# State products of the even heads on 48 instead of 64 columns of the turned keys, and one state bank that is cleared once

## The chip, the core and the metric

The kernel runs on one core of one Trainium2 chip. Times are microseconds on the device. The kernel before was measured three times: 484.71, 484.76 and 485.75 us, so the median is 484.76 us. One further execution was profiled. All durations below come from its trace.

## What is computed

An RWKV6 attention block is followed by an MLP mixer. The attention works on 4 sequences of 768 tokens, with 8 heads of 48 numbers each. For every head it carries a 48 x 48 state from token to token:

```
cur = einsum('bhd,bhe->bhde', u * k[t], v[t])
y[t] = einsum('bhd,bhde->bhe', r[t], state + cur)
state = w[t][..., None] * state + einsum('bhd,bhe->bhde', k[t], v[t])
```

The result, laid out as 4 x 768 x 384, goes through two matrix products over tokens and two over channels, each pair with a ReLU between them and a residual sum behind it.

## The kernel before

The attention is done in chunks of 64 tokens. A *unit* is 256 tokens of one sequence, so there are 12 units, three for each sequence. In a unit, `ends`, `keys`, `begins` and `queries` (L426 to L442) multiply the running products of `w` into the keys and queries. `tokens` (L471) then calls `turned_keys` (L337), which turns the keys so that the tokens stand on the partitions. `carry` (L486) calls `outer` (L352), which makes the products of turned keys and values. `update` and `scaled` (L492 to L512) carry the state from chunk to chunk, and `before` (L514) and `after` (L522) make the output.

Heads are kept in pairs. The even head of a pair has its 48 numbers on partitions 0 to 47 and the odd head on 64 to 111 (`P = 64`, `ROWS = 112`). Partitions 48 to 63 are padding, which holds zeros in the keys.

`turned_keys` turns each pair with a matmul against the identity (L343), and ScalarE copies 112 columns for each of four pairs out of PSUM into `kT` (L344). In a pair's 112 columns, 0 to 47 belong to the even head, 48 to 63 are padding and 64 to 111 belong to the odd head.

`outer` multiplies, for each pair of heads `a`, group of 128 tokens `c`, chunk `j` in it and head `q` of the pair, the turned keys (the operand that is loaded into the array) with 48 columns of values (the operand that streams through). The loaded operand takes the array's upper half of rows for `j` = 0 and the lower for `j` = 1, and the left half of columns for `q` = 0 and the right for `q` = 1. So the array works as four corners, one for each (j, q), and successive products go to different corners. The order is (0,0), (1,1), (0,1), (1,0). The even head loads 64 columns, its 48 and the 16 of padding. So it also writes partitions 48 to 63 of the state bank `kv_ps`, with zeros. The odd head loads 48 columns:

```
rows = slice(q * P, P + q * D)
```

A unit has 32 such products, or 24 in the last unit of a sequence, where the last chunk's state isn't needed. Each float32 product stands in the trace as two weight loads and two matmuls, called passes below: 8 units x 64 + 4 x 48 = 704 rows of each kind at L361.

In the first sequence, the state is carried in PSUM. ScalarE scales the state out of the bank (L497), and a matmul with the identity adds it back (L504) on all 112 rows. In later sequences VectorE adds it in SBUF (L512). Both read the padding rows too, which is why those must hold finite numbers. The bank comes from a pool of one buffer (`ps_a`), newly allocated in every `outer`, and once more by `back` (L893) of the first sequence's mixer.

The order of the work is written out by hand. For the first sequence it is the long `strict(...)` call (L1033). Later, `interleaved` (L1013) merges the pieces of the mixer of one sequence and of the attention of the next by the digits of `WEAVES`. Every engine works off its instructions in this order. ScalarE's first pieces are `masks` (L205), then `own_u` of unit 0 (L444, which issues at L329).

Of the kernel before, what the change touches and what calls it, by code (L numbers as in the profile page):

```python
# [10 lines left out]
f32 = mybir.dt.float32  # L11
# [9 lines left out]
B, H, S, D = 4, 8, 768, 48  # L21
DM = H * D
T = 64
C = S // 128
UC = 2
UB = C // UC
NU = B * UB
A = H // 2
P = 64
ROWS = P + D  # L30
# [35 lines left out]
def rwkv6_then_mixer(  # L66
# [18 lines left out]
    pe, dve, act, pool, sp = nc.tensor, nc.vector, nc.scalar, nc.gpsimd, nc.sync  # L85
# [32 lines left out]
    apool = ctx.enter_context(tc.tile_pool(name="apool", bufs=2))  # L118
# [4 lines left out]
    ps_a = ctx.enter_context(tc.tile_pool(name="ps_a", bufs=1, space=bass.MemoryType.PSUM))  # L123
# [3 lines left out]
    def bank(name):  # L127
        return ps_m.tile([128, 512], f32, name=name, tag="m")
# [18 lines left out]
    ident = const.tile([128, 128], f32, name="ident")  # L147
# [40 lines left out]
    load_w(0)  # L188
    act.dma_start(u_col, u)

    dve.memset(starts, 0.0)
    dve.memset(least, LEAST)
    dve.memset(most, -MOST)
# [11 lines left out]
    def masks():  # L205
        for j in range(2):
            act.copy(on_diagonal[ts(j, T)], ident[ts(j, T), ts(j, T)])
        act.copy(diagonal, on_diagonal)
        act.copy(before_it, strictly)

    wtok1 = wts.tile([128, C, DTOK], f32, name="wtok1")
    wtok2 = wts.tile([128, DTOK // 128, S], f32, name="wtok2")
# [123 lines left out]

    def turned_keys(k_):  # L337

        kT = apool.tile([128, UC, A, 128], f32, name="kT", bufs=1)
        both = [bank("k_ps").rearrange("p (a t) -> p a t", a=A) for c in range(UC)]  # L340
        for c in range(UC):
            for a in range(A):
                pe.transpose(both[c][:, a, :ROWS], k_[:ROWS, ts(c * A + a, 128)], ident[:ROWS, :ROWS])  # L343
        return kT, [lambda c=c: act.copy(kT[:, c, :, :ROWS], both[c][:, :, :ROWS]) for c in range(UC)]  # L344

    def all_turned(k_):
        kT, copies = turned_keys(k_)
        for f in copies:
            f()
        return kT  # L350

    def outer(kT, vt, half):  # L352

        kv = ps_a.tile([128, 2, 512], f32, name="kv_ps", tag="a")
        begun = set()
        for c in range(UC):
            for a in range(A):
                for j, q in ((0, 0), (1, 1), (0, 1), (1, 0)):
                    if 2 * (half * UC + c) + j < 2 * C - 1:
                        rows = slice(q * P, P + q * D)  # L360
                        pe.matmul(kv[rows, j, ds((c * A + a) * D, D)], kT[ts(j, T), c, a, rows],  # L361
                                  vt[ts(j, T), c, ts(2 * a + q, D)], start=(q, j) not in begun, stop=True, skip_group_check=True)
                        begun.add((q, j))
        return kv
# [40 lines left out]
    def unit(i):  # L405
# [80 lines left out]
        def carry():  # L486
            L["kv"] = outer(L.pop("kT"), vs[i], half)
# [61 lines left out]
    def slot(name, i, n=1):  # L549
        return room(name, *ROOMS[name])[:, ds(i * SLOT, n * SLOT)]  # L550
# [18 lines left out]
    def low_of_pair(kind, n):  # L569
        return source(kind, n) if kind else by_pair(kind, slot("forms3", 2 * n, 2))  # L570
# [52 lines left out]
    def left(kind, jt):  # L623
        up, joint = (by_pair(kind, form_of(kind, jt // 2, which)) for which in ("up", "joint"))
        if kind == 0:
            return [[t[:, m, ts(jt % 2, 128)] for m in range(3)] for t in (up, joint)]
        return [t[:, jt % 2] for t in (up, joint)]

    def join(to, high, low):
        dve.scalar_tensor_tensor(to, high.bitcast(f32), 1.0 / BASE, low.bitcast(f32), op0=ALU.mult, op1=ALU.add)  # L630
# [249 lines left out]
    def mixing(bt, x_of, out_rows, rounded=False):  # L880
        h1 = mpool.tile([128, DTOK // 128, DM], f32, name="h1", bufs=1)
        xT = mpool.tile([128, DM // 128, S], f32, name="xT", tag="xT", bufs=1)
        zs, sums = {}, {}

        def hidden(i, c):
            if c == 0:
                sums[i] = ps_m.tile([128, DM], f32, name="h1_ps", tag="m")
            pe.matmul(sums[i], now["wtok1"][:, c, ts(i, 128)], x_of()[:, c, :], start=(c == 0), stop=(c == C - 1))

        def rectified(i):  # L890
            act.activation(h1[:, i, :], sums.pop(i), AF.Relu)

        def back(c):  # L893
            if rounded and c == 0:
                ps = ps_a.tile([128, 2, 512], f32, name="h_ps", tag="a")[:, 0, :DM]
            else:
                ps = ps_m.tile([128, DM], f32, name="h_ps", tag="m")
            for i in range(DTOK // 128):
                pe.matmul(ps, now["wtok2"][:, i, ts(c, 128)], h1[:, i, :], start=(i == 0), stop=(i == DTOK // 128 - 1))
            x = x_of()  # L900
            dve.tensor_add(x[:, c, :], x[:, c, :], ps)

        def last_x():
            return [slot("x_forms", 2 * n, 2).rearrange("p (m t) -> p m t", m=3) for n in range(3)]

        def turn(c):

            ps = bank("xT_ps")[:, :DM].rearrange("p (m t) -> p m t", t=128)
            for m in range(DM // 128):
                pe.transpose(ps[:, m, :], x_of()[:, c, ts(m, 128)], ident)  # L910
            if not rounded or c < 4:
                act.copy(xT[:, :, ts(c, 128)], ps)
                return
            high, low, joint = (t[:, :, ts(c - 4, 128)] for t in last_x())
            act.mul(high, ps, UPWARD)
            dve.tensor_sub(low, ps, high.bitcast(f32))
            join(joint, high, low)

        def up(s, jt, blocks=range(DM // 128)):
            if jt == 0 and 0 in blocks:  # L920
                zs[s] = now["z"][int((bt, s) != (0, 0))].rearrange("p (j t) -> p j t", j=NJ)
            if 0 in blocks:
                sums["z", s] = ps_m.tile([128, SEG], f32, name="z_ps", tag="m")
            ps = sums["z", s]
            if rounded and s == 2:
                first, last = left(0, jt)
                low = low_of_pair(0, jt // 2)[:, :, ts(jt % 2, 128)]
                for n, (of, to) in enumerate(zip((first, [low[:, m] for m in range(3)], last), last_x())):
                    for m in range(3):
                        pe.matmul(ps, of[m], to[:, m], start=(n, m) == (0, 0), stop=(n, m) == (2, 2))  # L930
                act.activation(zs[s][:, jt, :], ps, AF.Relu, scale=1.0 - 1.0 / BASE)
                return
            for m in blocks:
                pe.matmul(ps, now["wch1"][:, m, ts(jt, 128)], xT[:, m, ts(s, SEG)],  # L934
                          start=(m == 0), stop=(m == DM // 128 - 1))
            if DM // 128 - 1 in blocks:
                act.activation(zs[s][:, jt, :], ps, AF.Relu)

        def down(s, n, jts):

            if jts[0] == 0:
                sums[n] = ps_m.tile([128, DM], f32, name="h2_ps", tag="m")
            ps = sums[n]
            for jt in jts:
                pe.matmul(ps, zs[s][:, jt, ts(n, 128)], now["wch2"][:, jt, :], start=(jt == 0), stop=(jt == NJ - 1))  # L945
            if jts[-1] == NJ - 1:
                o = mpool.tile([128, 2, DM], f32, name="o", bufs=1) if n == 0 else sums["o"]
                sums["o"] = o
                dve.tensor_add(o[:, n], x_of()[:, 2 * s + n, :], ps)
                sp.dma_start(out_rows(2 * s + n), o[:, n])  # L950

        return dict(hidden=hidden, rectified=rectified, xT=xT, back=back, turn=turn, up=up, down=down)

    now["z"] = halves
# [58 lines left out]
    def interleaved(order, *streams):  # L1013
# [17 lines left out]
    s0, s1, s2 = (e["updates"] for e in (e0, e1, e2))  # L1031
    t0, t1, t2 = (e["scaled"] for e in (e0, e1, e2))
    strict(lambda: load_part(0, 1), masks, e0["ends"], e0["own_u"][0], e0["own_u"][1], e0["own_u"][2], e0["own_u"][3], e0["begins"],  # L1033
           lambda: load_part(0, 0), e0["keys"], lambda: load_part(1, 1), e0["own_gram"], lambda: load_v(0), e0["ranges"][0], lambda: load_w(1),
           e0["tokens"], e0["queries"], e1["own_u"][0], e1["own_u"][1], e0["copied"][0], lambda: load_w(2), e0["gram"], e1["ends"], e0["copied"][1],
# [117 lines left out]
    def by_halves(b):  # L1153
# [17 lines left out]
        for half in range(UB):  # L1171
# [13 lines left out]
            for l in range(LEVELS):  # L1185
# [8 lines left out]
                decay = longer  # L1194
            by = decay[:ROWS].rearrange("p (x j) -> p x j", j=2)
            kv = outer(all_turned(k_), vt, half)
            for c in range(UC):
                for j in range(2):
# [82 lines left out]
```

## Time and profile before

| | |
|---|---|
| median of three runs | 484.76 us |
| span of the profiled execution | 484.2 us |
| TensorE matmul / weight load busy | 468.0 us (97%) / 411.1 us (85%) |
| VectorE / ScalarE / GpSimd busy | 336.4 / 254.3 / 59.3 us |
| matmuls of L361 in all (704) | 15.1 us with 64 columns, 13.5 us with 48 (they overlap) |
| ScalarE's copies to `kT` (24) | 12.1 us |

PE stands for TensorE's matmuls, PEld for its weight loads, DVE for VectorE, ACT for ScalarE, SP for the engine that issues most transfers. A row of groups names the line, the engine, the operation and the tiles (out<-in), for PE the rows and columns of the array that are used (64*48), then shapes and count. A row of the timeline begins with the start and the duration in us. A row of the chain of waits says which work ended last at each time. PEclk is the share of TensorE's full clock that was granted. It reads 1.00 where the trace has no record yet, at the very start.

### The profile page before, as it was taken

The page shows a single profiled execution, that of the slowest core. Times are in us where ns is not written, and L with a number is a line of the kernel's source. Part 1 is how long each engine was busy: PE and PEld are TensorE (multiplying, and loading weights), DVE is VectorE, ACT ScalarE, POOL GpSimd, SP SyncE. Part 2 cuts the span into 40 slices and gives each one's busy share as a digit, 9 for nine tenths or more (in the row PEclk, how much of TensorE's full clock was granted, in tenths as well). Part 3 has the DMA queues.
Part 4 walks back from the last instruction along what each step waited for, and adds up shares of the span by engine and source line. Part 5 has one row for each costly group of instructions (what it writes and reads, how often), then busy time and mean ns, then how long its engine had stood idle before and what let it go on. Part 6 is the DMA issues. An engine that isn't in the chain of part 4 may idle for free.

```text
span 484.2 us, 12668 instructions
## 1 busy us (share of the span) xinstructions
PE 468.0 (97%) x5298; PEld 411.1 (85%) x5298; DVE 336.4 (69%) x478; ACT 254.3 (53%) x587; POOL 59.3 (12%) x58
## 2 busy tenths in 40 slices
PE   3899999999999999999999999999999999999995
PEld 2786588866697668999999969999999979999995
DVE  7989799798778778766857298777856366235331
ACT  5679866664768665445446354355545234134140
POOL 1000000000000000320404002230313003032030
PEclk9769999999999999999999999999999999999999
DMA  8945946780574666864848653385615622436221
GB/s 311 316 146 199 265 165 189 256 261 32 162 238 126 204 181 188 249 205 134 245 118 256 213 164 113 129 241 192 190 33 167 224 83 81 115 100 200 91 85 56
DMA packets 49408, 83.77 MB, mean 173 GB/s; under 512 B 4864, under 2 KB 40576, under 8 KB 49344
## 3 DMA queue, kind: packets, MB, share of 16 engines
q1 hardware_dynamic: 49056, 82.80, 54.6%
q8 instruction: 43, 0.70, 0.6%
q14 instruction: 21, 0.17, 0.1%
q10 hardware_dynamic: 288, 0.10, 0.1%
HBM read 71.87 MB, written 11.01 MB: 171 GB/s over the span
## 4 chain that ended last, share of the span: by engine, by line
PE 93%; DMA 3%; ACT 2%; DVE 1%; SPq 1%; issue 0%; DVEq 0%; ACTq 0%
PE h_ps L945 10%; PE ends_ps L735 8%; PE ends_ps L742 8%; PE ends_ps L737 8%; PE o_ps L753 8%; PE o_ps L755 8%; PE o_ps L754 8%; PE z_ps L934 7%; PE h_ps L658 5%; PE gram L313 3%; PE z_ps L930 3%; PE h_ps L689 3%; PE y_ps L397 3%; PE y_ps L376 2%; PE kv_ps L361 2%; DMA w<-in_w_dram 2%
## 5 line engine op out<-in xcount | busy, mean ns | idle before, releaser
L728 POOL TENSOR_TENSOR z_high<-z_high 128x384 fp32r<-128x384 f32 x48 | 58.0, 1212 | 408.4 <-ACT z_high L717 190.8
L761 DVE SCALAR_TENSOR_TENSOR x<-o_ps,x 128x384 f32<-128x384 f32 x35 | 19.1, 555 | 55.5 <-PE o_ps L755 55.5
L717 ACT ACTIVATE z_high<-ends_ps 128x384 fp32r<-128x384 f32 x48 | 23.5, 489 | 58.1 <-PE ends_ps L742 58.1
L735 PE MATMUL ends_ps<-x_forms,forms 128*128 128x384 f32 x216 | 50.4, 341 | 0.0
L742 PE MATMUL ends_ps<-z_more,forms 128*128 128x384 f32 x216 | 50.2, 340 | 0.0
L737 PE MATMUL ends_ps<-x_forms,ring 128*128 128x384 f32 x216 | 49.3, 337 | 0.0
L945 PE MATMUL h_ps<-wch,z 128*128 128x384 f32 x144 | 48.6, 490 | 0.0
L724 DVE SCALAR_TENSOR_TENSOR z_high<-ends_ps,z_high 128x384 fp32r<-128x384 f32 x48 | 26.5, 553 | 31.0 <-ACT z_high L717 30.6
L753 PE MATMUL o_ps<-forms,z_high 128*128 128x384 f32 x140 | 47.9, 342 | 0.0
L755 PE MATMUL o_ps<-forms,z_high 128*128 128x384 f32 x140 | 47.2, 337 | 0.0
L754 PE MATMUL o_ps<-ring,z_high 128*128 128x384 f32 x140 | 47.1, 337 | 0.0
L497 ACT ACTIVATE before<-state,to_end 112x48 f32<-112x48 f32 x132 | 33.2, 323 | 18.2 <-DVE state L512 16.0
L945 PEld LDWEIGHTS h_ps<-wch,z 128*128 128x128 f32 x144 | 26.6, 190 | 16.8
L742 PEld LDWEIGHTS ends_ps<-z_more,forms 128*128 128x128 f32 x216 | 38.9, 188 | 0.3 <-DVE z_more L630 0.2
L735 PEld LDWEIGHTS ends_ps<-x_forms,forms 128*128 128x128 f32 x216 | 38.2, 188 | 0.7
L737 PEld LDWEIGHTS ends_ps<-x_forms,ring 128*128 128x128 f32 x216 | 38.5, 188 | 0.0
L934 PE MATMUL z_ps<-xT,wch 128*128 128x256 f32 x144 | 31.8, 380 | 0.0
L934 PEld LDWEIGHTS z_ps<-xT,wch 128*128 128x128 f32 x144 | 27.1, 190 | 3.8
L720 ACT ACTIVATE z_high<-z_high 128x384 fp32r<-128x384 f32 x48 | 25.2, 526 | 3.3
L753 PEld LDWEIGHTS o_ps<-forms,z_high 128*128 128x128 f32 x140 | 26.3, 188 | 0.2
L754 PEld LDWEIGHTS o_ps<-ring,z_high 128*128 128x128 f32 x140 | 26.3, 188 | 0.0
L755 PEld LDWEIGHTS o_ps<-forms,z_high 128*128 128x128 f32 x140 | 26.3, 188 | 0.0
(194 smaller groups left out, 936.5 us busy)
## 6 DMA issues: line engine op xcount, KB each, us to landing
ring<-third SPq DMA_DIRECT2D x144, 192.0 KB, 3.2
raw<-in_w_ch_dram SPq DMA_DIRECT2D x16, 512.0 KB, 5.0
rk<-in_rk_dram SPq DMA_DIRECT2D x36, 192.0 KB, 5.0
near<-in_near_dram SPq DMA_DIRECT2D x8, 768.0 KB, 4.8
w<-in_w_dram SPq DMA_DIRECT2D x10, 520.5 KB, 4.0
vt<-in_v_dram SPq DMA_DIRECT2D x12, 384.0 KB, 4.6
out_dram<-x SPq DMA_DIRECT2D x17, 192.0 KB, 2.3
third<-forms SPq DMA_DIRECT2D x12, 192.0 KB, 3.8
```

Source lines behind the costliest of these rows:

```text
L497: act.mul(t[:ROWS, a], state[bt, g][:ROWS, a], by_last(c, j)[:, a:a + 1])
L720: act.mul(z_form(jt, 2), z_form(jt, 0).bitcast(f32), 1.0 / BASE)
L724: dve.scalar_tensor_tensor(z_form(jt, 1), a, 0.0, z_form(jt, 0).bitcast(f32), op0=ALU.max, op1=ALU.subtract)
L728: pool.tensor_add(z_form(jt, 2), z_form(jt, 2).bitcast(f32), z_form(jt, 1).bitcast(f32))
L735: pe.matmul(a, up[m], xf[0][:, m], start=m == 0, stop=False)
L737: pe.matmul(a, low[:, m], xf[1][:, m], start=False, stop=False)
L742: pe.matmul(banks["a", jt], joint, xf[2][:, m], start=False, stop=m == 2)
L753: pe.matmul(a, z[0], up, start=first, stop=False, skip_group_check=True)
L754: pe.matmul(a, z[1], held[bt, s, half, 1, jt], start=False, stop=False, skip_group_check=True)
L755: pe.matmul(a, z[2], joint, start=False, stop=last, skip_group_check=True)
L934: pe.matmul(ps, now["wch1"][:, m, ts(jt, 128)], xT[:, m, ts(s, SEG)], start=(m == 0), stop=(m == DM // 128 - 1))
L945: pe.matmul(ps, zs[s][:, jt, ts(n, 128)], now["wch2"][:, jt, :], start=(jt == 0), stop=(jt == NJ - 1))
```

## The change

- `kv` is allocated once for the whole kernel. `outer` no longer allocates a bank, and `back` uses `kv` in place of its own tile.
- `masks` gets one ScalarE instruction more, which writes zeros into partitions 32 to 63 of both halves of the bank (1024 columns).
- `kT` keeps 96 columns for each pair instead of 128. The copy out of PSUM leaves the padding out, so it moves 4 x 2 x 48 = 384 columns instead of 448.
- The even heads' products load 48 columns instead of 64 and no longer write the padding rows.

No engine's instructions come in another order. Besides the new ScalarE instruction, only waits differ, all of them in the first sequence. The first product of units 1 and 2 no longer waits for TensorE's own earlier work (the old bank's). Five later TensorE instructions get such a wait in exchange, because that earlier wait had covered them: the first and the fifth turn of unit 2 (L343), the first two products of the mixer (L888) and the first product of unit 2's second Gram matrix (L313).

```diff
+    kv = ps_a.tile([128, 2, 512], f32, name="kv_ps", tag="a")
     dve.memset(starts, 0.0)
...
         act.copy(before_it, strictly)
+        act.mul(kv.rearrange("p j (m n) -> p (j m) n", n=128)[P // 2:P], ident[P // 2:P].unsqueeze(1).to_broadcast([P // 2, 8, 128]), 0.0)
...
-        kT = apool.tile([128, UC, A, 128], f32, name="kT", bufs=1)
+        kT = apool.tile([128, UC, A, 2 * D], f32, name="kT", bufs=1)
...
-        return kT, [lambda c=c: act.copy(kT[:, c, :, :ROWS], both[c][:, :, :ROWS]) for c in range(UC)]
+
+        def of_heads(t):
+            return t.rearrange("p a (q e) -> p a q e", q=2)[:, :, :, :D]
+
+        return kT, [lambda c=c: act.copy(kT[:, c].rearrange("p a (q e) -> p a q e", q=2), of_heads(both[c])) for c in range(UC)]
...
-        kv = ps_a.tile([128, 2, 512], f32, name="kv_ps", tag="a")
         begun = set()
...
                     if 2 * (half * UC + c) + j < 2 * C - 1:
-                        rows = slice(q * P, P + q * D)
-                        pe.matmul(kv[rows, j, ds((c * A + a) * D, D)], kT[ts(j, T), c, a, rows],
+                        pe.matmul(kv[q * P:q * P + D, j, ds((c * A + a) * D, D)], kT[ts(j, T), c, a, ts(q, D)],
...
-                ps = ps_a.tile([128, 2, 512], f32, name="h_ps", tag="a")[:, 0, :DM]
+                ps = kv[:, 0, :DM]
```

## The prediction

> **What bounds the kernel now.** I read the page's busy shares and its chain of waits first, then TensorE's waits, then the stage in which they lie.
>
> ```profile
> PE 468.0 (97%) x5298; PEld 411.1 (85%) x5298; DVE 336.4 (69%) x478; ACT 254.3 (53%) x587; POOL 59.3 (12%) x58
> ...
> PE 93%; DMA 3%; ACT 2%; DVE 1%; SPq 1%; issue 0%; DVEq 0%; ACTq 0%
> ```
>
> The chain that ended last runs over TensorE for 93% of the span. The table of windows shows where TensorE has room (columns: stretch, length, busy us and count of PE, PEld, DVE, ACT, POOL, clock, DMA):
>
> ```profile
> 8.30:24.00 15.70, 14.20 (x334) 12.14 (x338) 15.20 (x15) 11.11 (x31) 0.00 (x0) 0.84 0.96 342
> 24.00:48.00 24.00, 23.65 (x660) 18.62 (x656) 21.79 (x24) 19.48 (x56) 0.00 (x0) 0.82 0.53 170
> 48.00:479.00 431.00, 430.17 (x4312) 380.29 (x4312) 293.91 (x432) 220.21 (x494) 58.02 (x48) 1.00 0.54 167
> ```
>
> Of 431 us after 48, TensorE is busy for 430.17. What it waited for in that stretch, by the view of waits (total us, times, longest):
>
> ```profile
> PE h_ps L888 <- issue: 0.4, 1, 0.4
> PE h_ps L689 <- ACT z_high L682: 0.2, 1, 0.2
> ```
>
> So from 48 us on, a matmul that ends sooner brings the end forward by as much, unless another engine falls behind. VectorE and ScalarE have 137 and 211 us to spare there. Ahead of 24 us the chain is another one (start, us, what):
>
> ```profile
> 3.65 8.17 DMA w<-in_w_dram
> ...
> 14.55 5.50 DMA first<-in_rk_dram
> ...
> 22.22 0.42 ACT kT L344
> 22.64 1.05 ACT raw L263
> ...
> 23.79 0.34 PE y_ps L397
> ```
>
> There transfers and ScalarE decide, and TensorE work saved before 23.79 is lost. In the timeline, unit 0's products lie ahead of that point and those of units 1 to 11 behind it:
>
> ```profile
> 13.79 1.90 PE L361 MATMUL kv_ps<-vt,kT 64*64 64x48 f32 x64
> ...
> 25.54 1.92 PE L361 MATMUL kv_ps<-vt,kT 64*64 64x48 f32 x64
> ```
>
> **What the products cost.** First a group of 64 passes that all load 64 columns (the timeline), then unit 3's products, half of which load 48:
>
> ```profile
> 45.15 1.15 PE L397 MATMUL y_ps<-vt,at 64*64 64x48 f32 x64
> ```
>
> ```profile
> 82.34 1.09 PE L361 MATMUL kv_ps<-vt,kT 64*64 64x48 f32 x62
> 83.22 0.28 PE L313 MATMUL gram<-rk 48*64 48x64 f32 x2
> 83.25 0.24 PE L361 MATMUL kv_ps<-vt,kT 64*64 64x48 f32 x2
> ```
>
> Unit 3's group lasts from 82.34 to 83.49, 1.15 us, exactly as long as the group that loads 64 columns throughout. The 48-column half brings nothing so far: the left corners set the end. How fast each half could go is seen by counting the matmuls that had started by 82.44 and by 82.75 (one line's rows, from 82.3 on):
>
> ```profile
> L361 PE MATMUL kv_ps<-vt,kT x7: 205/240/254, 82.3 to 82.4; 64*48 64x48 f32 x4, 64*64 64x48 f32 x3
> ```
>
> ```profile
> L361 PE MATMUL kv_ps<-vt,kT x32: 205/218/254, 82.3 to 82.7; 64*48 64x48 f32 x18, 64*64 64x48 f32 x14
> ```
>
> In 0.31 us the two right corners began 14 passes with 48 columns, or 7 each: a step of 44 ns. The two left corners began 11 with 64 columns, 5.5 each: a step of 56 ns. So a corner's step follows the columns that it loads, and a narrow corner runs ahead of a wide one. Later it must wait for its turn, which is how both end together now. The weight loads of the same group give the difference again (busy us, mean ns of one):
>
> ```profile
> L361 PEld LDWEIGHTS kv_ps<-vt,kT 64*64 64x64 f32 x32 | 1.0, 135 | 0.3 <-issue 0.3
> L361 PEld LDWEIGHTS kv_ps<-vt,kT 64*48 64x48 f32 x32 | 0.9, 119 | 0.0
> ```
>
> 135 - 119 = 16 ns, against 56 - 44 = 12 by the counts. I take 13, near the counts, which measure starts. A corner has 8 products = 16 passes, so 15 steps: 15 x 13 = 195 ns, about **0.20 us a group**. A last unit of a sequence has 48 passes, but its upper corners still take 16 each, so it gains the same.
>
> Unit 1's group runs at half clock, which has its own counts (by 25.70 and by 26.35):
>
> ```profile
> L361 PE MATMUL kv_ps<-vt,kT x8: 277/290/303, 25.5 to 25.7; 64*64 64x48 f32 x4, 64*48 64x48 f32 x4
> ```
>
> ```profile
> L361 PE MATMUL kv_ps<-vt,kT x36: 277/290/310, 25.5 to 26.3; 64*48 64x48 f32 x20, 64*64 64x48 f32 x16
> ```
>
> 8 steps against 6 in 0.65 us, 81 against 108 ns: 15 x 27 = 0.40 us. But the clock comes back at a time of its own:
>
> ```profile
> 25.89:29.31 3.42, 3.42 (x99) 0.50 0.43 122
> 29.31:32.72 3.41, 3.41 (x49) 0.50 0.63 190
> 32.72:36.13 3.41, 3.41 (x166) 1.00 0.55 159
> ```
>
> If it still returns at 32.72, the work that is 0.40 us ahead then is worth only 0.20 us at the full clock. So unit 1 counts like the others: 11 x 0.20 = **2.2 us**.
>
> **The other parts.** *The clearing.* ScalarE's rows at the start are:
>
> ```profile
> 3.32 0.24 ACT L209 CAST before_it<-strictly 128x64 uint8<-128x64 f32 x1
> 7.04 1.71 ACT L329 ACTIVATE near<-rk,u_col 112x256 f32<-112x256 f32 x4 [3.48 <-DMA rk<-in_rk_dram]
> ```
>
> Its nearest row in size is 1024 columns of another activation:
>
> ```profile
> L263 ACT ACTIVATE raw<-raw,rebias 128x1024 uint16<-128x1024 uint16 x10 | 11.5, 1151 | 3.0 <-DVE raw L260 3.0
> ```
>
> So it lasts 1.15 us by that row, on fewer partitions and into PSUM, which no row shows at that size. It fits three times into the 3.48 us in which ScalarE waits for a transfer. Behind it on ScalarE stands only L329, which waits for the same transfer; without that cover L329, and TensorE's first products, would come 1.15 us later. Between 0 and 1.15, I take 0.
>
> *The narrower copy.* These rows say what 448 and 384 columns cost:
>
> ```profile
> L344 ACT COPY kT<-k_ps 128x448 f32<-128x448 f32 x24 | 12.1, 534 | 0.7 <-PE k_ps L343 0.6
> L403 ACT COPY x<-y_ps 128x384 f32<-128x384 f32 x12 | 5.7, 473 | 8.8 <-PE y_ps L397 8.8
> ```
>
> That is 61 ns for each of 24 copies, 1.5 us of ScalarE. One copy stands on the chain (22.22, above): 0.06 us. The other 23 lie beside TensorE's work, 0. If the gaps in its source held the copy at 534, the sum would lose the 0.06.
>
> *The waits.* Five TensorE instructions get a wait for TensorE's own work, two lose one. What they wait for is the former use of a PSUM bank, several groups back and done. The same wait stands today in the middle of unit 1's turns and not in unit 0's:
>
> ```profile
> 10.37 1.73 PE L343 MATMUL k_ps<-ident,rk 112*128 112x112 f32 x8
> ...
> 19.05 1.72 PE L343 MATMUL k_ps<-ident,rk 112*128 112x112 f32 x8 [0.18 <-PE kv_ps L504]
> ```
>
> 1.72 against 1.73 us: it costs 0. What is left if they do stop the queue is bounded by the 0.18 us of that row, 5 x 0.18 = 0.9. I take 0, the pair that differs in the wait alone. Queued behind them is all of TensorE's order, nothing else. No transfer moves, and no queue is passed.
>
> **The sum.** 2.2 + 0.06 = 2.26 us. The profiled execution spans 484.2, so 481.9. The median of the runs lies 0.56 above the span, and 484.76 - 2.26 = **482.5 us**. The step bounds give the ends: at 16 ns 11 x 15 x 16 = 2.64 us less, 482.1; at 12 ns 1.98 less, and with the waits at 0.9 it is 483.7.
>
> **The rivals.**
>
> *Starts in a row.* All four corners at 44 ns need a start every 11 ns. The counts show 25 starts in 0.31 us, 12.4 ns apart, and nothing closer over a stretch. If that is TensorE's pace, a step can't fall below 4 x 12.4 = 50 ns: 6 x 15 x 11 = 1.0 us, **483.8 us**. For it: no row is faster. Against it: at half clock the narrow corners got the 81 ns that their columns ask for, and in full clock their step lay at 44 from the start, so nothing pushed back.
>
> *The load isn't what paces.* If starts, or the streamed 48 columns, hold the step at 56 and the counts show only a shift in order, nothing comes: **484.7 us**. For it: group times of 1.15 with half of the loads narrow and with none. Against it: in the same 0.31 us 14 narrow and 11 wide started. Its sharpest form is in the Trainium skill, "TensorE: Matmul & The Clock Gate", section "Wait — 56ns, not 53.3ns?": matmul starts never come closer than about 25 ns, however few columns stream. By that page 64 passes take 1.6 us whatever they load, and the sum would be 0. The trace disagrees: 12.4 ns above, so I give this rival little.
>
> *The clock comes back later*, the case that could end slower. TensorE was busy for all 3.42 us of 25.89 to 29.31, and still got 0.50 in the next window. So busy time alone doesn't open the gate. If it goes by how much of the array works, loads of 48 columns in unit 1's group count for less. One window more at half clock costs 3.41 / 2 = 1.7 us, leaving 484.76 - 2.26 + 1.7 = **484.2**; two cost 3.4, **485.9**. It ends slower from a delay of 2 x 2.26 = 4.5 us on. The other way round, one window earlier (at 29.31) would give 484.76 - 2.26 - 1.7 = **480.8**. Against all of these: the window that did open the clock held 49 matmuls, fewer than the 99 of the one that didn't, so smaller products hardly decide. The Trainium skill's same page, section "What's actually happening", has the window free-running at 3413 ns and opening after one busy one. The trace agrees on the length, 3.41 us between the steps of its clock, and not on the one busy window. By that page's free phase the return could move by a window in any execution, of this kernel or the one before.
>
> **How the numbers follow.** Forecast (step by columns, 482.1 to 483.7): 0.70. Starts in a row: 0.12, of which half lies on each side of 0.2% (1.0 us, about what a measurement of this kernel can tell from no change). The load isn't what paces: 0.08. Clock one window later 0.04, two 0.03, one earlier 0.03. Faster: 0.70 + 0.06 + 0.03 = 0.79. Same: 0.06 + 0.08 + 0.04 = 0.18. Slower: 0.03. The range takes in the forecast, the starts in a row and one window later, up to 484.2. Below 482.1 it is widened by 0.5, half of the 1.0 us between the lowest and the highest run of before (484.71 and 485.75), to 481.6.
>
> **What would show it.** Right: L361 has 64*48 alone; a group of 64 passes lasts about 0.95 us in full clock and 1.5 in half; the copies to kT last some 475 ns; the clearing lies inside ScalarE's first wait; TensorE's waits after 48 us stay under 1 us. Wrong: a group still at 1.15, or nearer 1.05 (starts in a row); PEclk at 0.50 past 32.72; or a new wait of TensorE behind the shorter groups, which would mean that VectorE or ScalarE had less room than their busy shares say.

## The result, and the profile after

| | before | after |
|---|---|---|
| median of 22 runs each, side by side | 484.12 us (482.41 to 485.75) | 481.79 us (480.83 to 486.06) |
| profiled execution: span / its own time | 484.2 us / not listed | 480.5 us / 482.32 us |
| ratio after / before | | 0.9964, 95% interval [0.9952, 0.9976] |

The kernel became faster. The ratio stands for 1.7 us and its interval for 1.2 to 2.3 us. The medians lie 2.33 us apart (their quotient is 0.9952, and the ratio on record is not that quotient). The forecast change was 2.26 us.

The busy shares and the chain of waits, from the page of the kernel after:

```profile
PE 464.9 (97%) x5298; PEld 408.3 (85%) x5298; DVE 336.4 (70%) x478; ACT 254.0 (53%) x588; POOL 59.2 (12%) x58
...
PE 95%; ACT 2%; DMA 1%; issue 0%; SPq 0%; DVE 0%; DVEq 0%; ACTq 0%
```

TensorE is still the bound, and the other engines' busy times stand where they stood. TensorE has the same 5298 matmuls, with 3.1 us less of busy time. The table of windows shows the late stretch of the kernel after (stretch, length, busy us and count of PE, PEld, DVE, ACT, POOL, clock, DMA):

```profile
48.00:475.00 427.00, 426.74 (x4308) 377.47 (x4306) 292.83 (x429) 218.09 (x493) 57.98 (x48) 1.00 0.54 167
```

TensorE is idle for 0.26 us of 427. Its waits in that stretch, by the view of waits, are one:

```profile
PE h_ps L693 <- ACT z_high L686: 0.2, 1, 0.2
```

This wait stood there before, under L689. So the shorter groups met no new wait. The groups of products themselves, in the timeline of the kernel after (start, us, what): unit 1 at half clock, unit 2, unit 3 with what follows it, and unit 11:

```profile
26.09 1.50 PE L365 MATMUL kv_ps<-vt,kT 64*48 64x48 f32 x64
...
34.67 0.93 PE L365 MATMUL kv_ps<-vt,kT 64*48 64x48 f32 x48
...
80.50 0.94 PE L365 MATMUL kv_ps<-vt,kT 64*48 64x48 f32 x64
81.26 1.13 PE L315 MATMUL gram<-rk 48*64 48x64 f32 x64
82.31 2.86 PE L938 MATMUL z_ps<-xT,wch 128*128 128x256 f32 x12
...
350.18 0.90 PE L365 MATMUL kv_ps<-vt,kT 64*48 64x48 f32 x48
```

All products now use 48 columns (64*48). Unit 3's group lasts 0.94 us in place of 1.15, and unit 1's 1.50 in place of 1.92. The rows of that one group, from the view of one line, show the load and the matmul (count, then min/median/max ns, then first and last start):

```profile
L365 PEld LDWEIGHTS kv_ps<-vt,kT x64: 116/122/122, 80.5 to 81.2; 64*48 64x48 f32 x64
L365 PE MATMUL kv_ps<-vt,kT x64: 205/205/241, 80.5 to 81.2; 64*48 64x48 f32 x64
```

A single matmul lasts 205 ns at the median, where 205 to 254 stood in the prediction's rows of before. So what changed is above all how closely they start. Last, ScalarE's rows in the timeline of the kernel after, and its copies to `kT` in the groups (busy us, mean ns of one):

```profile
3.57 1.02 ACT L211 ACTIVATE kv_ps<-ident 32x1024 f32<-32x1024 f32 x1
6.66 1.71 ACT L331 ACTIVATE near<-rk,u_col 112x256 f32<-112x256 f32 x4 [2.07 <-DMA rk<-in_rk_dram]
```

```profile
L350 ACT COPY kT<-k_ps 128x384 f32<-128x384 f32 x24 | 10.8, 480 | 0.7 <-PE k_ps L345 0.7
```

The clearing takes 1.02 us and ends at 4.59. ScalarE then waits another 2.07 us for the transfer that it waited for before.

**Where the 3.7 us between the two profiled spans lie.** Each row gives how much later (+) or earlier (-) the same work starts in the kernel after. Unit 11's and unit 2's starts before, 353.62 and 35.66, are from the same timeline as unit 3's 82.34.

| at | before | after | difference | what came in between |
|---|---|---|---|---|
| first matmul of the output group at 24 us | 23.79 | 24.34 | +0.55 | mainly a stretch of full clock from 15.65 to 19.07 us, which of these two only the execution before has (below) |
| unit 2's products | 35.66 | 34.67 | -0.99 | unit 1's products, 0.42 shorter at half clock, and an earlier return of the full clock (29.5 against 32.7); the two were not told apart |
| unit 3's products | 82.34 | 80.50 | -1.84 | unit 2's products (0.2), TensorE's 0.4 us wait put down to "issue" at 48 us, which is not there after, and 0.2 in small pieces; the "issue" wait is not the change's, as run 11, the changed kernel again, has one of 0.76 us at 44.99 |
| unit 11's products | 353.62 | 350.18 | -3.44 | units 3 to 10: 271.28 against 269.68, **eight groups, 1.60 us** |
| end of the span | 484.2 | 480.5 | -3.7 | unit 11's products |

From unit 3 on, what the two profiles differ by is 0.20 us a group on average. Ahead of that, the two executions also differ in things that the change doesn't touch. The experiments separate the two.

One of these things is the chain ahead of 24 us. In the execution before it ran over transfers and ScalarE. In the one after, and in a second profile of the kernel before (run 12), it runs over TensorE and unit 0's products (start, us, what; first the kernel after, then run 12):

```profile
14.05 1.32 PE kv_ps L365 x63
```

```profile
14.09 1.72 PE kv_ps L361 x44
```

Another is the clock. The execution before has full clock from 15.65 to 19.07 us. In the one after, the records begin only at 29.5, but the same Gram group shows half clock there (the timelines of before and after):

```profile
17.20 1.16 PE L313 MATMUL gram<-rk,near 48*64 48x64 f32 x64
```

```profile
17.24 1.99 PE L315 MATMUL gram<-rk,near 48*64 48x64 f32 x64
```

### The profile page after: what moved, and what is told of

Read it like the earlier page. It is cut to its first block, busy times and chain, and to the rows that moved or that the text cites. A ratio compares the mean times of both kernels' runs of the same rounds, so it can differ in the third digit from the quotient of the medians.

```text
span 480.5 us, 12671 instructions
## 1 busy us (share of the span) xinstructions
PE 464.9 (97%) x5298; PEld 408.3 (85%) x5298; DVE 336.4 (70%) x478; ACT 254.0 (53%) x588; POOL 59.2 (12%) x58
## 4 chain that ended last, share of the span: by engine, by line
PE 95%; ACT 2%; DMA 1%; issue 0%; SPq 0%; DVE 0%; DVEq 0%; ACTq 0%
PE h_ps L949 10%; PE ends_ps L739 8%; PE ends_ps L746 8%; PE ends_ps L741 8%; PE o_ps L757 8%; PE o_ps L759 8%; PE o_ps L758 8%; PE z_ps L938 7%; PE h_ps L662 5%; PE gram L315 4%; PE z_ps L934 3%; PE h_ps L693 3%; PE y_ps L380 3%; PE y_ps L401 3%; PE kv_ps L365 2%; PE k_ps L345 2%
## 5 line engine op out<-in xcount | busy, mean ns | idle before, releaser
L938 PEld LDWEIGHTS z_ps<-xT,wch 128*128 128x128 f32 x144 | 27.1, 190 | 3.8
```

## The experiments

The theory was the forecast's: a corner's step follows the columns that it loads. The rivals were starts in a row (no step under 50 ns), a load that doesn't set the pace, and one that came with the first profile after: that the bank allocated once, its clearing or the narrower copy gives or takes time. All edits are to the changed kernel. A group is read by two numbers: the time from its first to its last start, and its whole length in the timeline.

**1. The wide loads alone put back.** The bank is still allocated once and cleared, but copy and loads are those of before.

```diff
-        kT = apool.tile([128, UC, A, 2 * D], f32, name="kT", bufs=1)
+        kT = apool.tile([128, UC, A, 128], f32, name="kT", bufs=1)
...
-        return kT, [lambda c=c: act.copy(kT[:, c].rearrange("p a (q e) -> p a q e", q=2), of_heads(both[c])) for c in range(UC)]
+        return kT, [lambda c=c: act.copy(kT[:, c, :, :ROWS], both[c][:, :, :ROWS]) for c in range(UC)]
...
-                        pe.matmul(kv[q * P:q * P + D, j, ds((c * A + a) * D, D)], kT[ts(j, T), c, a, ts(q, D)],
+                        rows = slice(q * P, P + q * D)
+                        pe.matmul(kv[rows, j, ds((c * A + a) * D, D)], kT[ts(j, T), c, a, rows],
```

> The changed kernel with the wide loads put back: one bank, cleared once, but 64 columns for the even heads and the copy of 448 columns. Theory (a corner of the array steps at the pace of the columns that it loads, and the slowest corner ends the group): a group of 64 passes in full clock lasts 1.15 us from first to last end again (0.93 to the last start), and the time is that of the kernel before, ratio 0.998 to 1.002. Rival (the single bank or its waits bring part of the gain): groups at 1.15, but the ratio stays at 0.998 or less.

Measured: 484.75 us (12 runs) against 484.06 (17 runs) of the kernel before, ratio 1.0014 [0.9999, 1.0028]. The timeline of this run:

```profile
81.85 1.07 PE L363 MATMUL kv_ps<-vt,kT 64*64 64x48 f32 x61
...
82.76 0.24 PE L363 MATMUL kv_ps<-vt,kT 64*64 64x48 f32 x2
82.81 1.13 PE L315 MATMUL gram<-rk 48*64 48x64 f32 x62
83.87 2.42 PE L936 MATMUL z_ps<-xT,wch 128*128 128x256 f32 x10
```

The group is back at 82.76 + 0.24 - 81.85 = 1.15 us, and unit 3 to unit 11 takes 353.12 - 81.85 = 271.27 us, as before. With the loads wide again the whole gain is gone. So it comes from the loads (or the copy, below) and not from the bank. The interval leaves room for a cost of the bank of up to 1.4 us, which runs 7 to 11 take up.

**2. One corner of four wide.** Only the products of (j, q) = (0, 0) load 64 columns; copy and `kT` are as in run 1.

```diff
+                        rows = slice(q * P, q * P + (P if (j, q) == (0, 0) else D))
+                        pe.matmul(kv[rows, j, ds((c * A + a) * D, D)], kT[ts(j, T), c, a, rows],
```

> One corner in four loads 64 columns (even head, first chunk of 64 tokens), the other three 48. Theory (each corner keeps its own pace, the slowest ends the group): last start 0.93 us after the first and 1.15 us in all, as with two wide corners, so the whole gain is lost in each group. Rival (the loads share one path and their sum counts): a quarter of the gain is lost, last start at 0.73 + 0.05 to 0.10 = 0.78 to 0.83 us, 0.98 to 1.03 in all.

Measured: last start after 0.91 us, and by the timeline of this run:

```profile
79.78 1.07 PE L363 MATMUL kv_ps<-vt,kT 64*64 64x48 f32 x63
...
80.69 0.22 PE L363 MATMUL kv_ps<-vt,kT 64*64 64x48 f32 x1
```

80.69 + 0.22 - 79.78 = 1.13 us. One wide corner costs 0.19 of the 0.21 us that two cost, and unit 3 to unit 11 takes 350.98 - 79.78 = 271.20 us, near the 271.28 of two. The corners don't share the cost; the slowest one sets the end of the group. (One run: 483.13 us.)

**3. 32 columns loaded.** The products leave out 16 of each head's 48 rows of the state, which stay zero; a second clearing covers the rows 96 to 127.

```diff
+        act.mul(kv.rearrange("p j (m n) -> p (j m) n", n=128)[96:128], ident[96:128].unsqueeze(1).to_broadcast([P // 2, 8, 128]), 0.0)
...
-                        pe.matmul(kv[q * P:q * P + D, j, ds((c * A + a) * D, D)], kT[ts(j, T), c, a, ts(q, D)],
+                        pe.matmul(kv[q * P:q * P + 32, j, ds((c * A + a) * D, D)], kT[ts(j, T), c, a, ds(q * D, 32)],
```

> All four corners load 32 of the 48 columns, so rows 32 to 47 of each head's state stay zero (that part of the state is left out); a second clearing covers the odd heads' rows. Theory (columns set the step, 13 ns for 16 of them): the step goes from 45 to 32 ns, last start at 0.73 - 15 x 0.013 = 0.53 us, about 0.73 us in all. Rival 1 (the 48 streamed columns set the step by now): last start stays at 0.73. Rival 2 (starts in a row at 12.4 ns): stays at 0.73 too, with starts evenly apart; as the changed kernel starts four passes 7 ns apart and then pauses 26, rival 2 has little left.

Measured: last start after 0.68 us, not 0.53. By the timeline of this run:

```profile
80.63 0.88 PE L366 MATMUL kv_ps<-vt,kT 64*32 64x48 f32 x64
81.44 1.16 PE L316 MATMUL gram<-rk 48*64 48x64 f32 x64
82.53 3.72 PE L939 MATMUL z_ps<-xT,wch 128*128 128x256 f32 x16
```

Here the theory fell in its plain form. From 64 to 48 columns a group shortened by 0.20 us, from 48 to 32 by 0.05. The stretch from unit 3 to unit 11 even grew, from 269.68 to 270.43 us. Two explanations were open: a floor on starts (four starts in 43 ns, 10.7 ns each), or the 48 columns that stream. (483.22 us, one run.)

**4. Narrow loads, wide copy.** The copy and `kT` of before, with 48 columns loaded from them.

```diff
+                        rows = slice(q * P, q * P + D)
+                        pe.matmul(kv[rows, j, ds((c * A + a) * D, D)], kT[ts(j, T), c, a, rows],
```

> The changed kernel with the old copy to kT (448 columns, padding included) and narrow loads taken from it. Theory: groups as in the changed kernel (0.73 us to the last start), copies at 534 ns instead of 480, and a span within what two executions differ by, since the copies lie beside TensorE. Rival (the copies matter): the stretch from 48 us on is longer by up to 18 x 0.054 = 1.0 us.

Measured, from the timeline and from the groups of this run:

```profile
79.83 0.94 PE L363 MATMUL kv_ps<-vt,kT 64*48 64x48 f32 x64
```

```profile
L347 ACT COPY kT<-k_ps 128x448 f32<-128x448 f32 x24 | 12.1, 534 | 0.6 <-PE k_ps L345 0.6
```

The copies last 534 ns again, the group 0.94 us, and unit 3 to unit 11 takes 269.69 against 269.68 us. From unit 3 on, the copies' 54 ns are hidden. (481.69 us, one run.)

**5. 48 columns loaded, 32 streamed**, and **6. both 32.** They separate the two explanations of run 3. Both leave out a third of the value columns, the second also a third of the state's rows; the whole bank is cleared, so that what isn't written is zero.

```diff
-        act.mul(kv.rearrange("p j (m n) -> p (j m) n", n=128)[P // 2:P], ident[P // 2:P].unsqueeze(1).to_broadcast([P // 2, 8, 128]), 0.0)
+        act.mul(kv.rearrange("p j (m n) -> p (j m) n", n=128), ident.unsqueeze(1).to_broadcast([128, 8, 128]), 0.0)
...
-                        pe.matmul(kv[q * P:q * P + D, j, ds((c * A + a) * D, D)], kT[ts(j, T), c, a, ts(q, D)],
-                                  vt[ts(j, T), c, ts(2 * a + q, D)], start=(q, j) not in begun, stop=True, skip_group_check=True)
+                        pe.matmul(kv[q * P:q * P + D, j, ds((c * A + a) * D, 32)], kT[ts(j, T), c, a, ts(q, D)],
+                                  vt[ts(j, T), c, ds((2 * a + q) * D, 32)], start=(q, j) not in begun, stop=True, skip_group_check=True)
```

Run 6 has `kv[q * P:q * P + 32, ...]` and `kT[..., ds(q * D, 32)]` besides.

> 48 columns loaded as in the changed kernel, but only 32 of the 48 columns of values streamed (so 16 columns of each head's state stay zero, that part of the state is left out); the clearing covers the whole bank. The run that loaded 32 and streamed 48 stopped at a step of 43 ns instead of 32. New theory (a corner's step is the longer of its load and its stream): the load still asks for 45 ns, last start stays at 0.73 us. Rival (the stream alone sets the step since the loads have 48 columns): the step falls to about 30 ns, last start about 0.5 us.

> 32 columns loaded and 32 streamed (rows and columns 32 to 47 of each head's state are left out). New theory (the longer of load and stream): the step falls to 45 - 13 = 32 ns, last start at 15 x 0.032 + 0.05 = 0.53 us or less, about 0.74 us in all. Rival (a floor under the starts, near the 43 ns of the run that loaded 32 columns, that is 10.8 ns from start to start): last start stays at 0.68 us.

Measured, by the timelines of run 5 and of run 6:

```profile
79.93 0.92 PE L365 MATMUL kv_ps<-vt,kT 64*48 64x32 f32 x64
```

```profile
78.41 0.76 PE L365 MATMUL kv_ps<-vt,kT 64*32 64x32 f32 x64
79.10 1.16 PE L315 MATMUL gram<-rk 48*64 48x64 f32 x64
80.19 6.09 PE L938 MATMUL z_ps<-xT,wch 128*128 128x256 f32 x27
```

Neither size alone shortens the step by much, both together do: 0.94, 0.92 and 0.88 us for 48/48, 48 loaded and 32 streamed, 32 loaded and 48 streamed, and 0.76 for 32/32. So a corner's step goes by the longer of its load and its stream, and there is no floor at 10.7 ns a start. The gaps between the first starts of unit 3's group say the same (ns, from the trace's records; four starts, one in each corner, make a step):

```
64 and 48 loaded, 48 streamed (run 1)   6  7  7 66   8  0 19 18   8 13 19  5 ...
48 loaded, 48 streamed (after)          7  7  6 61   6  8  5 26   6  8  5 26 ...
48 loaded, 32 streamed (run 5)          6  7  7 46   6  8  5 26   6  8  5 26 ...
32 loaded, 48 streamed (run 3)          7  7  6 47   7  7  6 22   7  8  5 23 ...
32 loaded, 32 streamed (run 6)          7  7  6 33   7  7  6 12   6  8  6 11 ...
```

The mean step after the first is (last start - first step - 20) / 14, 20 ns being what the fourth corner starts behind the first one (7 + 7 + 6): (930 - 86 - 20) / 14 = 59 ns, (730 - 81 - 20) / 14 = 45, (715 - 66 - 20) / 14 = 45, (682 - 67 - 20) / 14 = 42, (564 - 53 - 20) / 14 = 35. Run 6 begins with steps of 32 and ends nearer 34, so there something else than 32 columns begins to count; what it is stays open. (481.83 and 479.68 us, one run each.)

**7 to 11. What the clearing costs.** Run 7, repeated as run 10, takes ScalarE's clearing away and lets VectorE do it. Run 9 clears twice on ScalarE. Runs 8 and 11 are the changed kernel again.

```diff
     dve.memset(ones, 1.0)
+    dve.memset(kv[P // 2:P], 0.0)
...
-        act.mul(kv.rearrange("p j (m n) -> p (j m) n", n=128)[P // 2:P], ident[P // 2:P].unsqueeze(1).to_broadcast([P // 2, 8, 128]), 0.0)
```

```diff
-        act.mul(kv.rearrange("p j (m n) -> p (j m) n", n=128)[P // 2:P], ident[P // 2:P].unsqueeze(1).to_broadcast([P // 2, 8, 128]), 0.0)
+        for _ in range(2):
+            act.mul(kv.rearrange("p j (m n) -> p (j m) n", n=128)[P // 2:P], ident[P // 2:P].unsqueeze(1).to_broadcast([P // 2, 8, 128]), 0.0)
```

> The changed kernel with the padding rows cleared by VectorE at the start, not by ScalarE. Theory (the clearing lies inside ScalarE's wait for the first keys and costs nothing): same time as the changed kernel, 481.8 us, ratio to before 0.9950 to 0.9965. Rival (the single bank's clearing costs the 0.14% by which the kernel with wide loads lay above before): ratio lower by 0.001 or more than that of the changed kernel on the same chip.

> The changed kernel once more, beside the run with VectorE's clearing on the same chip. Theory (11 groups, each 0.20 us shorter): 2.2 us less than before, ratio 0.9954, within 0.9940 to 0.9970. Rival (something in the bank or its waits gives part of it back): ratio at 0.9970 or more.

> The changed kernel with ScalarE's clearing done twice, 2.0 us in all, which still ends inside ScalarE's wait for the first keys. Theory (hidden): the time of the changed kernel on the same chip, ratio to before within 0.0012 of its. Rival (the clearing costs something of its own, 0.3 to 0.7 us): the ratio is higher than that of the changed kernel by 0.0006 to 0.0015.

> VectorE's clearing again. Theory (where the clearing stands makes no difference): ratio to before as the changed kernel's on the same chip, within 0.0012. Rival (ScalarE's clearing costs): lower by 0.0012 or more, as the first comparison suggested (0.9946 against 0.9963).

> The changed kernel as the measure for the two runs above. Theory (11 groups of 0.20 us): ratio to before 0.9954, within 0.9940 to 0.9970.

| run | clearing | median, us | runs | before beside it | ratio to before |
|---|---|---|---|---|---|
| 8 | ScalarE, once | 481.76 | 12 | 483.89 | 0.9963 [0.9947, 0.9978] |
| 7 | VectorE | 481.34 | 6 | 483.89 | 0.9946 [0.9928, 0.9964] |
| 11 | ScalarE, once | 482.12 | 6 | 484.36 | 0.9945 [0.9927, 0.9963] |
| 10 | VectorE | 481.74 | 6 | 484.36 | 0.9951 [0.9933, 0.9969] |
| 9 | ScalarE, twice | 481.54 | 5 | 484.36 | 0.9940 [0.9925, 0.9956] |

Run 7 missed what was expected of it: at 0.9946 it lies below its range, and 0.0017 below run 8, where 0.001 was to speak for a cost of the clearing. Run 10, the same kernel, lies 0.0006 above run 11, so that difference did not come again. All five intervals overlap. Twice the clearing costs no more than once (0.9940 against 0.9945), and with none on ScalarE no saving can be told. ScalarE's rows in the timeline of run 9 show why:

```profile
3.57 2.07 ACT L212 ACTIVATE kv_ps<-ident 32x1024 f32<-32x1024 f32 x2
6.60 1.71 ACT L332 ACTIVATE near<-rk,u_col 112x256 f32<-112x256 f32 x4 [0.96 <-DMA rk<-in_rk_dram]
```

Even two clearings end before the transfer does, with 0.96 us to spare. So the clearing costs nothing. For the rest of the bank (its waits) there is run 1, with the room that its interval leaves.

**12. The kernel before, profiled again**, without any edit. It asks which part of the 3.7 us between the two spans belongs to the change.

> A second profile of the kernel before, as the first differs from that of the changed kernel by 3.7 us of span where the runs differ by 2.3. Theory (the first 48 us vary from execution to execution with the granted clock, the rest does not): from the start of unit 3's products to that of unit 11's again 271.3 us, and the start of unit 3's products anywhere from 80.5 to 82.4 us, so a span between 482.3 and 484.3. Rival (the change shortens the rest by more than its groups): that stretch differs from 271.3 by over 0.3 us.

Measured: 484.5 us span, 486.34 us its own time. Its timeline, and its windows around the clock's return:

```profile
82.52 1.07 PE L361 MATMUL kv_ps<-vt,kT 64*64 64x48 f32 x61
...
83.43 0.24 PE L361 MATMUL kv_ps<-vt,kT 64*64 64x48 f32 x2
83.49 1.13 PE L313 MATMUL gram<-rk 48*64 48x64 f32 x62
84.55 1.78 PE L934 MATMUL z_ps<-xT,wch 128*128 128x256 f32 x7
```

```profile
25.89:29.31 3.42, 3.42 (x100) 2.87 (x96) 3.42 (x4) 2.83 (x8) 0.00 (x0) 0.50 0.44 122
29.31:32.72 3.41, 3.41 (x47) 3.19 (x40) 2.43 (x4) 1.74 (x6) 0.00 (x0) 0.50 0.65 211
32.72:36.13 3.41, 3.41 (x164) 2.80 (x166) 3.01 (x4) 2.69 (x10) 0.00 (x0) 0.99 0.50 137
```

Unit 3 starts at 82.52 and the span is 484.5, both just outside what was expected. Unit 3 to unit 11 takes 271.29 us, so the late part repeats to 0.01 us here (and to 0.06 in three executions of the changed kernel: 269.68, 269.71 in run 8, 269.74 in run 11). Ahead of unit 3 this execution is as slow as the first profiled one: the clock comes back at the same place.

## Why the prediction held, point by point

**The time: the change was right, the starting point was not.** 2.26 us were forecast, and the medians lie 2.33 apart. But 482.5 us were forecast and 481.79 measured. Of these 0.71 us, 0.64 is the starting point: the three runs of before had a median of 484.76, the 22 have 484.12. So the time lies below the 482.1 to 483.7 of the mechanism. It stays inside the range by 0.19 us, and only because the range was widened to 481.6 for the spread of those three runs.

**A corner's step follows the columns that it loads: right, with a limit.** The step taken was 56 against 44 ns; it is 59 against 45. The 13 ns chosen became 14, and a group 0.20 us shorter, as the sum had it: 1.60 us over eight groups. Run 1 shows that this is the loads' doing. What the forecast did not know is that the 48 streamed columns are almost as long as the 48 loaded ones (42 and 45 ns). The change stops near where the stream takes over, which run 3 found and runs 5 and 6 explained. The Trainium skill, "TensorE: Matmul & The Clock Gate", section "LDWEIGHTS (loading the stationary operand)", puts a load at its columns divided by 1.2, in ns. That gives, as an estimate, 53 for 64 and 40 for 48. The trace agrees with the difference, 14 against 13, and lies 5 to 6 ns above both.

**Unit 1 at half clock: the size was right.** 0.40 us was worked out and 1.92 - 1.50 = 0.42 came. The mean step went from (1614 - 87 - 20) / 14 = 108 to (1220 - 80 - 20) / 14 = 80 ns.

**Starts in a row: wrong.** This rival took 12.4 ns from start to start as TensorE's pace. In the kernel after, 64 starts lie in 0.73 us, 11.6 ns apart, and in run 6 in 0.56 us, 9.0 ns apart. The 12.4 was the mean of the corners' own steps, 25 starts in 0.31 us.

**The load isn't what paces: wrong at 64 columns.** Run 1 against the kernel after decides it. In a weaker form it came true at 48: fewer columns loaded bring almost nothing there (run 3), since the stream holds the step. The 25 ns between starts that the prediction cites with this rival (the Trainium skill, "TensorE: Matmul & The Clock Gate", section "Wait — 56ns, not 53.3ns?") do not hold here, at 48 streamed columns in four corners: starts lie 11.6 ns apart on average, and 5 to 8 within a step.

**Clearing, copy, waits: next to nothing, as costed.** The clearing took 1.02 us (1.15 estimated) inside ScalarE's wait; doubled, it still cost nothing. The copies took 480 ns (473 estimated), and run 4 shows from unit 3 on that no part of their 54 ns reaches the end. The 0.06 us ahead of 24 us is too small to tell. The five added waits stand between 30.40 and 40.11 us in the kernel after (L345, L892, L315). TensorE's waits there, from 24 to 60 us, are one, and it is for ScalarE:

```profile
PE kv_ps L508 <- ACT before L501: 0.2, 1, 0.2
```

Run 1, which has all five, has 1.0 in its interval. That interval alone doesn't exclude the 0.9 us that bounded them. Nor was the 0.18 us behind it a bound: that wait in unit 1's turns, which the change leaves, lasted 1.01 us in run 8.

**Unit 0's products: put at nothing from one execution.** The prediction called TensorE's work ahead of 23.79 us lost, as the chain of its one profile ran over transfers and ScalarE there. In the kernel after and in run 12 the chain runs over unit 0's products, which last 1.50 us after and 1.90 before, at half clock. So in some executions a twelfth group can count, with up to 0.40 us. No run tells how often, and the medians' differences, 2.13 to 2.33 us, do not settle it.

**The clock's return: the step that failed, without moving the forecast.** The sum took the return at 32.72 us as fixed (a window later or earlier stood among the rivals), and the profiled execution as 0.56 us below the median, which set a span against the runs' own times. Both were wrong. In the records of TensorE's clock, the full clock comes back for good at 32.7 and 32.8 in the two profiles of the kernel before, at 32.9 in run 1, at 29.5 in the kernel after, between 27.1 and 28.2 in runs 2 to 5 and 7 to 9, at 25.9 in run 11 and at 20.8 in run 6. In run 10 it is there from the first record on, at 11.9, and unit 1's products run at full clock:

```profile
24.93 0.94 PE L365 MATMUL kv_ps<-vt,kT 64*48 64x48 f32 x64 [0.41 <-ACT before L501]
```

And a run's own time lies about 1.8 us above its span (482.32 with 480.5, 486.34 with 484.5). So the execution that was profiled took, as an estimate, 486.0 us, almost 2 us over the median of 22 runs of before (484.12). The sum came out right because 2.26 was taken off the median and not off that execution.

Does the change bring the clock back sooner? The three profiles with two wide corners have it late and the others earlier, which looks like a cause. Three things speak against it. First, executions of one and the same kernel differ more: runs 7 and 10 have one kernel, with the clock back at 27.1 and by 11.9 us, and the changed kernel had it at 29.5, 27.7 (run 8) and 25.9 (run 11). Second, the two profiled executions of the kernel before are late ones. They lie about 2 us over the medians, and their mean granted clock of 0.985 is below that of all 45 other executions of it that are listed with one (0.989 to 1.000, where a stretch without a record counts as 1.00). Third, a return 3.2 us earlier (32.7 to 29.5) is worth half of that, 1.6 us. On top of the loads' 2.2 it makes 3.8 us, about what lies between the two profiled executions (486.0 and 482.32), and about what the prediction's rival of one window earlier would bring. The medians differ by 2.33, 2.13 (483.89 - 481.76) and 2.24 us (484.36 - 482.12), and the loads alone account for these. A smaller shift stays open, as no run varied the return by itself.

## What to carry to other kernels

When small matmuls go round the corners of the array, count the starts of each corner over a stretch. The slowest corner sets the end of the group: here one corner left wide cost 0.19 of the 0.21 us that two cost. Work out the step of the load and that of the stream, since here an operand made smaller paid only down to the other one. And take a small forecast off the median of many runs, not of three, and read the gain from stretches that repeat (here unit 3 to unit 11, to 0.01 us before and 0.06 after). One profiled execution was 2 us off, and its chain ahead of 24 us was not that of the next one.

## What the runs showed of the hardware that had not been expected

**Behind products that load 32 columns, the next group starts later.** In the kernel after, the Gram group starts 0.76 us after the products do (80.50 to 81.26), 0.03 after their last start at 0.73. With 32 columns loaded it starts 0.81 - 0.68 = 0.13 us after it (80.63 to 81.44, run 3), and with 32 of both 0.69 - 0.56 = 0.13 us (78.41 to 79.10, run 6). With 48 loaded and 32 streamed it is 0.77 - 0.72 = 0.05 us (79.93 to 80.70, run 5), so this goes with the load. What the array does in that time, no run shows. From the products' start to the line after the Gram group it takes 82.31 - 80.50 = 1.81 us in the kernel after, 1.90 in run 3 and 1.78 in run 6; with the wide loads it takes 2.02 (run 1) and 2.03 (run 12). So run 6, whose products are 0.18 us shorter than those of the kernel after, gains 0.03 us a group: its stretch from unit 3 to unit 11 is 269.34 against 269.68 us.

**A narrow corner runs ahead.** The prediction's counts, 18 matmuls of narrow corners and 14 of wide ones begun after 0.41 us, come again in run 1 (its line's rows up to 82.26):

```profile
L363 PE MATMUL kv_ps<-vt,kT x32: 205/218/254, 81.8 to 82.3; 64*48 64x48 f32 x18, 64*64 64x48 f32 x14
```

By its gaps above, the starts cease to come in fours after the first step, and those of the kernel after, with all corners alike, never do.

**The full clock was back for good at 11.9 to 32.9 us**, in kernels that differ little ahead of it, and by 27.1 and 11.9 us in two executions of one kernel (runs 7 and 10). In the second profile of the kernel before TensorE was busy for all of 25.89 to 29.31 and still had 0.50 in the next window, as in the first.
